# Moving the last full-array weight group of a squared-ReLU MLP to row tiles, and cutting the last output tile in two pieces in place of three

## The chip, the cores and the metric

The kernel runs on one core of a Trainium2 chip. The metric is the device time of one execution in microseconds (us), lower is better. One profiled execution gives a trace; its span is about 1.8 us less than the measured time of the same execution.

The lines of the profile use short names: PE is TensorE's matmuls, PEld its weight loads, ACT ScalarE, DVE VectorE, POOL GpSimd, SPq the DMA queue of SyncE; L182 is line 182 of the kernel.

## The reference

```python
B, S, D, F = 1, 2048, 576, 4608          # all bfloat16
h = einsum("bsd,df->bsf", x, w1) + b1    # contraction over D = 576
h = relu(h) ** 2
out = einsum("bsf,fd->bsd", h, w2) + b2  # contraction over F = 4608
```

## The kernel before

D = 576 is 4.5 times 128. A contraction over 576 therefore leaves a half slice of 64 rows. The kernel deals with it in two ways, and the change is about the choice between them.

The 2048 rows are four blocks of 512. The 4608 columns of w1 are 36 f-tiles of 128. For 32 of them the array is used as two *row tiles*: two f-tiles are computed at once, one on the upper 64 rows of the array and one on the lower 64, in nine slices of 64 each.

```python
def a_rows(sb, ...):                     # 16 groups of two f-tiles
    for j in range(NJ):                  # NJ = 16
        bx = ps_h.tile(...); by = ps_h.tile(...)
        for i in range(NC):              # NC = 9 slices of 64
            matmul(bx, lhsT=w1_h[0:H, LO_C[i], jc], rhs=xT[0:H, LO_W[i], :], ...)   # upper half
            matmul(by, lhsT=w1_h[H:P, UP_C[i], jc], rhs=xT[H:P, UP_W[i], :], ...)   # lower half
        evac_h(sb, bx, G + j)            # ScalarE: relu(x + b1); VectorE: square -> hT
        evac_h(sb, by, G + NJ + j)
```

The other four f-tiles (G = 4) form the *full-array group*: four matmuls over 128 rows for each f-tile, and the left-over 64 rows of two f-tiles as one pair of half-array matmuls.

```python
def a_full(sb, order):                   # four f-tiles
    def pair(i, start, stop):            # the left-over 64 rows of two f-tiles
        matmul(banks[2*i],   lhsT=w1n8[0:H, i, :], rhs=xT[0:H, SPC, :], ...)
        matmul(banks[2*i+1], lhsT=w1n8[H:P, i, :], rhs=xT[H:P, E3, :], ...)
    def full(g, k, start, stop):         # 128 rows
        matmul(banks[g], lhsT=w1n[:, k, g*P:(g+1)*P], rhs=xT[:, O + k, :], ...)
    # ... three orders: "k_outer" (block 0), "rows_first" (blocks 1, 3), "g_outer" (block 2)
```

The second product has two parts. `phase_t` makes output columns 512 to 575 of two blocks at once, with the array cut in two *column tiles* (128 rows by 64 columns). `phase_b` makes columns 0 to 511 with the full array. The very last tile of 128 output rows is cut by columns, so that its last addition and store are small.

```python
EDGES = [0, 224, 384, 512]
def phase_b(sb, hT, last=False, ...):
    for jj in range(RT):
        edges = EDGES if last and jj == RT - 1 else [0, DM]       # DM = 512
        for d0, d1 in zip(edges, edges[1:]):
            po = ps_o.tile(...)
            for i, ft in enumerate(ft_order):                     # 36 f-tiles
                matmul(po[:, 0:d1-d0], lhsT=hT[:, ft, jj*P:(jj+1)*P], rhs=w2_sb[:, ft, d0:d1], ...)
            tensor_tensor(out=o_sb[:, d0:d1], in0=po[:, 0:d1-d0], in1=b2_bc[:, d0:d1], op=add)
            dma_start(out=out2[rt*P:(rt+1)*P, d0:d1], in_=o_sb[:, d0:d1])
```

The order of the phases:

```python
a_full(0, "k_outer"); a_rows(0, 12, 1)
a_rows(1); a_full(1, "rows_first")
phase_t(0); phase_b(0, ...); phase_b(1, ...)
a_full(2, "g_outer"); a_rows(2)
a_rows(3); a_full(3, "rows_first")
phase_t(2); phase_b(2, ...); phase_b(3, ..., last=True)
```

Of the kernel before, what the change touches and what calls it, by code (L numbers as in the profile page):

```python
# [11 lines left out]
BF16 = mybir.dt.bfloat16  # L12
# [5 lines left out]
def kernel(  # L18
# [9 lines left out]
    nc = tc.nc  # L28
    keep = tc.keep_in_program_order
    P = 128  # L30
    H = 64
# [5 lines left out]
    NC = D // H  # L37
    NK = NC // 2
    G = 4
    GW = G * P  # L40
    NJ = (NFT - G) // 2
# [8 lines left out]
    wpool = ctx.enter_context(tc.tile_pool(name="wpool", bufs=1))  # L50
# [15 lines left out]
    w1n = wpool.tile([P, NK, GW], BF16, name="w1n")  # L66
    w1n8 = wpool.tile([P, G // 2, P], BF16, name="w1n8")
    w1_h = wpool.tile([P, NC, FH], BF16, name="w1_h")
    w1_v = w1.rearrange("(c p) f -> p c f", p=H)

    def load_x(eng, rt):
        keep(eng.dma_start(out=xs[:, rt, :], in_=x2[rt * P:(rt + 1) * P, :]))
# [8 lines left out]
    def load_w1(eng, h, j0, j1):  # L81
        keep(eng.dma_start(out=w1_h[h * H:(h + 1) * H, :, j0 * P:j1 * P],
                      in_=w1_v[:, :, GW + h * FH + j0 * P:GW + h * FH + j1 * P]))

    load_x(nc.sync, 0)
    load_x(nc.scalar, 1)
# [20 lines left out]
    E3, O, SPC, E = 0, 1, 5, 6  # L107
    LO_W = [O, O + 1, O + 2, O + 3, E, E + 1, E + 2, E3, SPC]
    LO_C = [0, 2, 4, 6, 1, 3, 5, 7, 8]
    UP_W = [O, O + 1, O + 2, O + 3, E3, E, E + 1, E + 2, SPC]  # L110
    UP_C = [1, 3, 5, 7, 8, 2, 4, 6, 0]
# [6 lines left out]
    def dup_windows(sb):  # L118
        xT = xT_blk[sb]
        keep(nc.vector.tensor_copy(out=xT[0:H, SPC:SPC + 4, :], in_=xT[H:P, E3:E3 + 4, :]))  # L120
        keep(nc.vector.tensor_copy(out=xT[H:P, SPC:SPC + 4, :], in_=xT[0:H, O:O + 4, :]))  # L121
# [34 lines left out]
    def make_b1T():  # L156
        b1T_ps = ps_o.tile([P, P], BF16, name="b1T_ps", tag="po")
        keep(nc.tensor.transpose(b1T_ps[:], b1_rows[:], ident[:]))  # L158
        keep(nc.vector.tensor_copy(out=b1T[:], in_=b1T_ps[:, 0:NFT]))
# [3 lines left out]
    def alloc_hT(sb):  # L163
        hTs[sb] = hpool.tile([P, NFT, SB], BF16, name="hT", tag="hT")

    def evac_h(sb, bank, ft):
        r = rpool.tile([P, SB], BF16, name="r", tag="r")
        keep(nc.scalar.activation(out=r[:], in_=bank[:], func=ACT.Relu, bias=b1T[:, ft:ft + 1], scale=1.0))  # L168
        keep(nc.vector.tensor_tensor(out=hTs[sb][:, ft, :], in0=r[:], in1=r[:], op=ALU.mult))  # L169

    def a_rows(sb, dup_at=None, dup_sb=None):
        xT = xT_blk[sb]
        for j in range(NJ):
            if j == dup_at:
                dup_windows(dup_sb)
            bx = ps_h.tile([P, SB], FP32, name="ph", tag="ph")
            by = ps_h.tile([P, SB], FP32, name="ph", tag="ph")
            jc = slice(j * P, (j + 1) * P)
            for i in range(NC):
                keep(nc.tensor.matmul(bx[:], lhsT=w1_h[0:H, LO_C[i], jc], rhs=xT[0:H, LO_W[i], :],  # L180
                                 start=(i == 0), stop=(i == NC - 1)))
                keep(nc.tensor.matmul(by[:], lhsT=w1_h[H:P, UP_C[i], jc], rhs=xT[H:P, UP_W[i], :],  # L182
                                 start=(i == 0), stop=(i == NC - 1)))
            evac_h(sb, bx, G + j)
            evac_h(sb, by, G + NJ + j)

    def a_full(sb, order):
        xT = xT_blk[sb]
        banks = []
        for g in range(G):  # L190
            pool, tag = (ps_o, "po") if g < 2 else (ps_h, "ph")
            banks.append(pool.tile([P, SB], FP32, name="pn", tag=tag))

        def pair(i, start, stop):
            keep(nc.tensor.matmul(banks[2 * i][:], lhsT=w1n8[0:H, i, :], rhs=xT[0:H, SPC, :],  # L195
                             start=start, stop=stop))
            keep(nc.tensor.matmul(banks[2 * i + 1][:], lhsT=w1n8[H:P, i, :], rhs=xT[H:P, E3, :],  # L197
                             start=start, stop=stop))

        def full(g, k, start, stop):  # L200
            keep(nc.tensor.matmul(banks[g][:], lhsT=w1n[:, k, g * P:(g + 1) * P], rhs=xT[:, O + k, :],  # L201
                             start=start, stop=stop))

        if order == "rows_first":
            for i in (1, 0):
                pair(i, True, False)
            for g in (2, 3, 0, 1):
                for k in range(NK):
                    full(g, k, False, k == NK - 1)
                evac_h(sb, banks[g], g)  # L210
        else:
            if order == "k_outer":
                for k in range(NK):
                    for g in range(G):
                        full(g, k, k == 0, False)
                    if k == 1:
                        make_b1T()
            else:
                for g in (2, 3, 0, 1):
                    for k in range(NK):  # L220
                        full(g, k, k == 0, False)
            for i in (1, 0):
                pair(i, False, True)
                evac_h(sb, banks[2 * i], 2 * i)
                evac_h(sb, banks[2 * i + 1], 2 * i + 1)

    ft_order = list(range(G))
    for j in range(NJ):
        ft_order += [G + j, G + NJ + j]

    t_order = ft_order[G:] + ft_order[:G]
    EDGES = [0, 224, 384, 512]

    def phase_t(sb):
        pt = ps_o.tile([P, SB], FP32, name="pt", tag="po")
        for i, ft in enumerate(t_order):
            for h in range(2):
                keep(nc.tensor.matmul(pt[h * DT:(h + 1) * DT, :], lhsT=w2_sb[:, ft, DM:D], rhs=hTs[sb + h][:, ft, :],  # L238
                                      start=(i == 0), stop=(i == NFT - 1)))
        oT = tpool.tile([P, SB], BF16, name="oT", tag="oT")  # L240
        keep(nc.scalar.activation(out=oT[:], in_=pt[:], func=ACT.Identity, bias=b2T[:], scale=1.0))  # L241
        ot = tpool.tile([P, RT, P], BF16, name="ot", tag="ot")
        keep(nc.sync.dma_start_transpose(out=ot[:, :, :], in_=oT[:, :]))
        for h in range(2):
            r0 = (sb + h) * SB
            dst = out2[r0:r0 + SB, DM:D].rearrange("(j p) d -> p j d", p=P)
            keep(nc.sync.dma_start(out=dst, in_=ot[:, :, h * DT:(h + 1) * DT]))

    def phase_b(sb, hT, last=False, dups=()):
        for jj in range(RT):  # L250
# [3 lines left out]
            o_sb = opool.tile([P, DM], BF16, name="o_sb", tag="o_sb")  # L254
            edges = EDGES if last and jj == RT - 1 else [0, DM]
            for d0, d1 in zip(edges, edges[1:]):
# [7 lines left out]
    for (j0, j1) in [(0, 1), (1, 2), (2, 4), (4, 6), (6, 8), (8, 10), (10, 12)]:  # L264
        load_w1(nc.sync, 0, j0, j1)
        load_w1(nc.sync, 1, j0, j1)
    load_xT(1)
    for (j0, j1) in [(12, 14), (14, 16)]:
        load_w1(nc.sync, 0, j0, j1)
        load_w1(nc.sync, 1, j0, j1)  # L270
    keep(nc.sync.dma_start(out=b2_bc[:], in_=b2.partition_broadcast(P)))
    for c in (0, 3, 1, 4, 2, 5):
        load_w2(c)
    load_xT(2)

    alloc_hT(0)
    a_full(0, "k_outer")
    a_rows(0, 12, 1)
    alloc_hT(1)
    load_xT(3)  # L280
    a_rows(1)
    a_full(1, "rows_first")
    phase_t(0)
    phase_b(0, hTs[0], dups=(2, 3))
    phase_b(1, hTs[1])
    alloc_hT(2)
    a_full(2, "g_outer")
    a_rows(2)
    alloc_hT(3)
    a_rows(3)  # L290
    a_full(3, "rows_first")
    phase_t(2)
    phase_b(2, hTs[2])
    phase_b(3, hTs[3], last=True)
# [30 lines left out]
```

## Time and profile before

| | before |
|---|---|
| time, first three runs | 291.56 us median (291.02 to 291.71) |
| span of the profiled run | 289.7 us |
| TensorE matmul busy | 285.7 us, 99% |
| ScalarE, VectorE busy | 95.7 us, 79.7 us |
| chain of waits | 98% TensorE |

These are lines of the page of the kernel before: busy time of each engine, then the chain of work that ended last, then the costliest groups (line, engine, operation, output<-inputs, shape, count | busy us, mean ns of one | idle time before them).

```profile
span 289.7 us, 4742 instructions
PE 285.7 (99%) x2052; PEld 134.1 (46%) x2052; DVE 79.7 (28%) x175; ACT 95.7 (33%) x156; POOL 4.2 (1%) x13
...
PE 98%; ACT 0%; DVE 0%; issue 0%
...
L182 PE MATMUL ph<-xTw,w_h 64*128 64x512 bf16 x576 | 124.6, 376 | 0.0
L180 PE MATMUL ph<-xTw,w_h 64*128 64x512 bf16 x576 | 124.6, 376 | 0.0
```

TensorE is the bound and has no idle time to fill. The two row-tile groups show how such a page has to be read: both are busy for 124.6 us, but at the same time. A matmul is listed with 376 ns, but the next one on the same half starts 0.22 us after it (below); what counts is the time from one start to the next. So the timeline is the view for this kernel. Its columns are the start in us, the duration, the engine, the line, the instruction (output<-inputs, shape) and how many are merged in the line; square brackets give the idle time before it and what ended that. In the kernel before, at the end of block 1's row tiles:

```profile
72.16 0.38 PE L195 MATMUL pn<-xTw,w1n_92 64*128 64x512 bf16 x1
72.16 0.38 PE L197 MATMUL pn<-xTw,w1n_92 64*128 64x512 bf16 x1
72.38 0.38 PE L195 MATMUL pn<-xTw,w1n_92 64*128 64x512 bf16 x1
72.38 0.38 PE L197 MATMUL pn<-xTw,w1n_92 64*128 64x512 bf16 x1
72.69 0.60 PE L201 MATMUL pn<-xTw,w1n 128*128 128x512 bf16 x2
...
75.72 0.59 PE L201 MATMUL pn<-xTw,w1n 128*128 128x512 bf16 x2
76.25 0.41 PE L238 MATMUL pt<-hT,w_sb 128*64 128x512 bf16 x2
```

Two halves start together, and the next pair 0.22 us later (72.16, 72.38). Where the layout of the array changes, the next start comes after 0.31 us: from row tiles to the full array at 72.38 to 72.69, and again from the full array (the second of the two at 75.72, so about 75.94) to column tiles at 76.25.

The tail of the same run, in the timeline of all engines:

```profile
279.04 0.69 DVE L261 TENSOR_TENSOR o_sb<-po,b_bc 128x512 bf16<-128x512 f32 x1 [7.08 <-PE po L259]
...
282.49 0.39 DVE L261 TENSOR_TENSOR o_sb<-po,b_bc 128x224 bf16<-128x224 f32 x1 [2.76 <-PE po L259]
284.98 0.33 DVE L261 TENSOR_TENSOR o_sb<-po,b_bc 128x160 bf16<-128x160 f32 x1 [2.10 <-PE po L259]
286.99 0.29 DVE L261 TENSOR_TENSOR o_sb<-po,b_bc 128x128 bf16<-128x128 f32 x1 [1.69 <-PE po L259]
```

Each addition starts when the 36 matmuls of its piece are done. The three pieces therefore take 3.45, 2.49 and 2.01 us.

### The profile page before, as it was taken

To read this page: it belongs to the slowest core of one execution; us is meant where nothing else is said; L and a number is where in the kernel's file an instruction comes from. 1 tells how busy PE (TensorE), PEld (TensorE's weight loads), DVE (VectorE), ACT (ScalarE), POOL (GpSimd) and SP (SyncE) were. 2 spreads that over 40 slices of the span, in tenths; PEclk is the share of its full clock that TensorE was granted. 3 is DMA by queue.
4 is the path that set the end of the run, shared out by engine and by line. 5 is a ranking of instruction groups with operands and counts; after the bars stand their busy time and mean duration, and the time that the engine had idled before them with its cause. 6 is when DMAs were issued, how large, how long until landed. Compare 5 with 4: busy or idle time off the path is not lost.

```text
span 289.7 us, 4742 instructions
## 1 busy us (share of the span) xinstructions
PE 285.7 (99%) x2052; PEld 134.1 (46%) x2052; DVE 79.7 (28%) x175; ACT 95.7 (33%) x156; POOL 4.2 (1%) x13
## 2 busy tenths in 40 slices
PE   8999999999999999999999999999999999999996
PEld 4444444444444444444444444444445444444475
DVE  3444554444502100000025444444440000000001
ACT  4566666666500000000027666666670000000000
POOL 5000000000000000000000000000000000000000
PEclk9999999999999999999999999999999999999999
DMA  7999999400001000000000000000000100000000
GB/s 205 253 227 208 316 391 157 95 0 2 0 20 36 0 18 20 18 18 18 20 18 2 1 2 0 2 0 2 0 2 0 36 20 18 18 18 20 18 20 20
DMA packets 30501, 16.26 MB, mean 56 GB/s; under 512 B 14692, under 2 KB 30448, under 8 KB 30480
## 3 DMA queue, kind: packets, MB, share of 16 engines
q1 hardware_dynamic: 30032, 15.59, 22.4%
q8 instruction: 16, 0.26, 0.4%
q10 hardware_dynamic: 288, 0.30, 0.3%
q0 software_dynamic: 160, 0.08, 0.1%
q14 instruction: 5, 0.04, 0.0%
HBM read 11.36 MB, written 2.36 MB: 47 GB/s over the span
## 4 chain that ended last, share of the span: by engine, by line
PE 98%; ACT 0%; DVE 0%; issue 0%
PE po L259 43%; PE ph L180 42%; PE pt L238 5%; PE pn L201 5%; PE wps L63 1%; PE ph L182 1%; PE pn L195 1%; PE ta L145 0%; ACT xTw L150 0%; ACT xTw L151 0%; DVE o_sb L261 0%; PE tb L149 0%; PE tb L148 0%; PE b1T_ps L158 0%; PE pn L197 0%
## 5 line engine op out<-in xcount | busy, mean ns | idle before, releaser
L259 PE MATMUL po<-w_sb,hT 128*128 128x512 bf16 (+3 forms) x648 | 124.8, 355 | 0.0
L182 PE MATMUL ph<-xTw,w_h 64*128 64x512 bf16 x576 | 124.6, 376 | 0.0
L180 PE MATMUL ph<-xTw,w_h 64*128 64x512 bf16 x576 | 124.6, 376 | 0.0
L168 ACT ACTIVATE r<-ph,b1T 128x512 bf16<-128x512 f32 x128 | 81.1, 685 | 41.6 <-PE ph L182 41.6
L259 PEld LDWEIGHTS <-hT 128*128 128x128 bf16 x648 | 60.7, 98 | 64.3 <-issue 0.8
L180 PEld LDWEIGHTS <-w_h 64*128 64x128 bf16 x576 | 54.1, 94 | 68.3
L169 DVE TENSOR_TENSOR hT<-r 128x512 bf16<-128x512 bf16 x144 | 61.3, 426 | 77.3 <-ACT r L168 76.9
L182 PEld LDWEIGHTS <-w_h 64*128 64x128 bf16 x576 | 54.1, 94 | 0.0
L261 DVE TENSOR_TENSOR o_sb<-po,b_bc 128x512 bf16<-128x512 f32 (+3 forms) x18 | 11.4, 633 | 125.0 <-PE po L259 125.0
L168 ACT ACTIVATE r<-pn,b1T 128x512 bf16<-128x512 f32 x16 | 10.3, 688 | 70.5 <-PE pn L197 69.2
L238 PE MATMUL pt<-hT,w_sb 128*64 128x512 bf16 x144 | 15.9, 380 | 0.0
L201 PE MATMUL pn<-xTw,w1n 128*128 128x512 bf16 x64 | 14.5, 379 | 0.4 <-ACT xTw L150 0.4
L238 PEld LDWEIGHTS <-w_sb 128*64 128x64 bf16 x144 | 8.0, 110 | 7.8 <-issue 0.8
L201 PEld LDWEIGHTS <-w1n 128*128 128x128 bf16 x64 | 6.0, 98 | 8.2 <-issue 1.4
L241 ACT ACTIVATE oT<-pt,b2T 128x512 bf16<-128x512 f32 x2 | 1.4, 687 | 14.5 <-PE pt L238 14.5
L63 PE MATMUL wps<-const-bfloat16-1.0 128*128 128x512 bf16 (+1 forms) x7 | 2.9, 594 | 0.8 <-PEq L309 0.8
L120 DVE COPY xTw<-xTw 64x2048 bf16<-64x2048 bf16 x4 | 2.8, 690 | 0.4 <-ACT xTw L151 0.3
L121 DVE COPY xTw<-xTw 64x2048 bf16<-64x2048 bf16 x4 | 2.7, 686 | 0.1
L146 DVE COPY xTw<-ta 128x384 bf16<-128x384 bf16 x4 | 1.4, 358 | 4.5 <-PE ta L145 4.3
L195 PE MATMUL pn<-xTw,w1n_92 64*128 64x512 bf16 x8 | 2.4, 379 | 0.0
L197 PE MATMUL pn<-xTw,w1n_92 64*128 64x512 bf16 x8 | 2.4, 379 | 0.0
L63 PEld LDWEIGHTS <-const-bfloat16-1.0 128*128 128x128 bf16 x7 | 0.9, 135 | 2.1 <-issue 2.1
(26 smaller groups left out, 16.1 us busy)
## 6 DMA issues: line engine op xcount, KB each, us to landing
w_sb<-in_w_dram SPq DMA_DIRECT2D x6, 864.0 KB, 10.6
w_h<-in_w_dram SPq DMA_DIRECT2D x14, 288.0 KB, 6.3
out_dram<-o_sb SPq DMA_DIRECT2D x15, 128.0 KB, 1.7
w_h<-in_w_dram SPq DMA_DIRECT2D x4, 144.0 KB, 3.5
w1n<-in_w_dram SPq DMA_DIRECT2D x4, 128.0 KB, 3.7
x_sb<-in_x_dram ACTq DMA_DIRECT2D x2, 144.0 KB, 3.2
x_sb<-in_x_dram SPq DMA_DIRECT2D x2, 144.0 KB, 2.9
out_dram<-ot SPq DMA_DIRECT2D x4, 64.0 KB, 1.9
```

The lines of the kernel that those rows point to most:

```text
L63: keep(nc.tensor.matmul(wps[:, 0:n], lhsT=ones[:, 0:P], rhs=ones[:, 0:n], start=True, stop=True))
L120: keep(nc.vector.tensor_copy(out=xT[0:H, SPC:SPC + 4, :], in_=xT[H:P, E3:E3 + 4, :]))
L121: keep(nc.vector.tensor_copy(out=xT[H:P, SPC:SPC + 4, :], in_=xT[0:H, O:O + 4, :]))
L168: keep(nc.scalar.activation(out=r[:], in_=bank[:], func=ACT.Relu, bias=b1T[:, ft:ft + 1], scale=1.0))
L169: keep(nc.vector.tensor_tensor(out=hTs[sb][:, ft, :], in0=r[:], in1=r[:], op=ALU.mult))
L180: keep(nc.tensor.matmul(bx[:], lhsT=w1_h[0:H, LO_C[i], jc], rhs=xT[0:H, LO_W[i], :], start=(i == 0), stop=(i == NC - 1)))
L182: keep(nc.tensor.matmul(by[:], lhsT=w1_h[H:P, UP_C[i], jc], rhs=xT[H:P, UP_W[i], :], start=(i == 0), stop=(i == NC - 1)))
L195: keep(nc.tensor.matmul(banks[2 * i][:], lhsT=w1n8[0:H, i, :], rhs=xT[0:H, SPC, :], start=start, stop=stop))
L201: keep(nc.tensor.matmul(banks[g][:], lhsT=w1n[:, k, g * P:(g + 1) * P], rhs=xT[:, O + k, :], start=start, stop=stop))
L238: keep(nc.tensor.matmul(pt[h * DT:(h + 1) * DT, :], lhsT=w2_sb[:, ft, DM:D], rhs=hTs[sb + h][:, ft, :], start=(i == 0), stop=(i == NFT - 1)))
L259: keep(nc.tensor.matmul(po[:, 0:d1 - d0], lhsT=hT[:, ft, jj * P:(jj + 1) * P], rhs=w2_sb[:, ft, d0:d1], start=(i == 0), stop=(i == NFT - 1)))
L261: keep(nc.vector.tensor_tensor(out=o_sb[:, d0:d1], in0=po[:, 0:d1 - d0], in1=b2_bc[:, d0:d1], op=ALU.add))
```

## The change

The intent is one way of working in place of two. The full-array group stays only in block 0, where it starts TensorE on the first weights to arrive. In blocks 1 to 3 the same four f-tiles run as two more row-tile groups; for that their weights are loaded a second time, in row-tile layout (`w1_x`). The last tile is cut into 384 and 128 columns in place of 224, 160 and 128.

```diff
+    w1_x = wpool.tile([P, NC, GW // 2], BF16, name="w1_x")
+    def load_w1x(eng, h):
+        keep(eng.dma_start(out=w1_x[h * H:(h + 1) * H, :, :], in_=w1_v[:, :, h * GW // 2:(h + 1) * GW // 2]))
     ...
     def a_rows(sb, dup_at=None, dup_sb=None):
-        for j in range(NJ):
+        pairs = [] if sb == 0 else [(w1_x, j, j, G // 2 + j) for j in range(G // 2)]
+        pairs += [(w1_h, j, G + j, G + NJ + j) for j in range(NJ)]
+        for n, (w, j, fa, fb) in enumerate(pairs):
     ...          # a_full: only the order "k_outer" is left
-    t_order = ft_order[G:] + ft_order[:G]        # phase_t now uses ft_order
-    EDGES = [0, 224, 384, 512]
+    EDGES = [0, 384, 512]
     ...          # after the loads of w1_h, ahead of b2 and w2:
+    for h in range(2):
+        load_w1x(nc.sync, h)
     ...
     a_rows(1)
-    a_full(1, "rows_first")
     phase_t(0)
     ...
-    a_full(2, "g_outer")
     a_rows(2)
     a_rows(3)
-    a_full(3, "rows_first")
     phase_t(2)
```

More of the change, by code (lines that the diff above doesn't have):

```diff
@@ L172, in a_rows @@
         xT = xT_blk[sb]
-        for j in range(NJ):
-            if j == dup_at:
+        pairs = [] if sb == 0 else [(w1_x, j, j, G // 2 + j) for j in range(G // 2)]
+        pairs += [(w1_h, j, G + j, G + NJ + j) for j in range(NJ)]
+        for n, (w, j, fa, fb) in enumerate(pairs):
+            if n == dup_at:
                 dup_windows(dup_sb)
@@ L179, in a_rows, with a_full @@
             for i in range(NC):
-                keep(nc.tensor.matmul(bx[:], lhsT=w1_h[0:H, LO_C[i], jc], rhs=xT[0:H, LO_W[i], :],
+                keep(nc.tensor.matmul(bx[:], lhsT=w[0:H, LO_C[i], jc], rhs=xT[0:H, LO_W[i], :],
                                  start=(i == 0), stop=(i == NC - 1)))
-                keep(nc.tensor.matmul(by[:], lhsT=w1_h[H:P, UP_C[i], jc], rhs=xT[H:P, UP_W[i], :],
+                keep(nc.tensor.matmul(by[:], lhsT=w[H:P, UP_C[i], jc], rhs=xT[H:P, UP_W[i], :],
                                  start=(i == 0), stop=(i == NC - 1)))
-            evac_h(sb, bx, G + j)
-            evac_h(sb, by, G + NJ + j)
-    def a_full(sb, order):
+            evac_h(sb, bx, fa)
+            evac_h(sb, by, fb)
+    def a_full(sb):
         xT = xT_blk[sb]
@@ L192, in a_full @@
             banks.append(pool.tile([P, SB], FP32, name="pn", tag=tag))
-        def pair(i, start, stop):
+        for k in range(NK):
+            for g in range(G):
+                keep(nc.tensor.matmul(banks[g][:], lhsT=w1n[:, k, g * P:(g + 1) * P], rhs=xT[:, O + k, :],
+                                 start=(k == 0), stop=False))
+            if k == 1:
+                make_b1T()
+        for i in (1, 0):
             keep(nc.tensor.matmul(banks[2 * i][:], lhsT=w1n8[0:H, i, :], rhs=xT[0:H, SPC, :],
-                             start=start, stop=stop))
+                             start=False, stop=True))
             keep(nc.tensor.matmul(banks[2 * i + 1][:], lhsT=w1n8[H:P, i, :], rhs=xT[H:P, E3, :],
-                             start=start, stop=stop))
-        def full(g, k, start, stop):
-            keep(nc.tensor.matmul(banks[g][:], lhsT=w1n[:, k, g * P:(g + 1) * P], rhs=xT[:, O + k, :],
-                             start=start, stop=stop))
-        if order == "rows_first":
-            for i in (1, 0):
-                pair(i, True, False)
-            for g in (2, 3, 0, 1):
-                for k in range(NK):
-                    full(g, k, False, k == NK - 1)
-                evac_h(sb, banks[g], g)
-        else:
-            if order == "k_outer":
-                for k in range(NK):
-                    for g in range(G):
-                        full(g, k, k == 0, False)
-                    if k == 1:
-                        make_b1T()
-            else:
-                for g in (2, 3, 0, 1):
-                    for k in range(NK):
-                        full(g, k, k == 0, False)
-            for i in (1, 0):
-                pair(i, False, True)
-                evac_h(sb, banks[2 * i], 2 * i)
-                evac_h(sb, banks[2 * i + 1], 2 * i + 1)
+                             start=False, stop=True))
+            evac_h(sb, banks[2 * i], 2 * i)
+            evac_h(sb, banks[2 * i + 1], 2 * i + 1)
     ft_order = list(range(G))
@@ L229 @@
         ft_order += [G + j, G + NJ + j]
-    t_order = ft_order[G:] + ft_order[:G]
-    EDGES = [0, 224, 384, 512]
+    EDGES = [0, 384, 512]
     def phase_t(sb):
         pt = ps_o.tile([P, SB], FP32, name="pt", tag="po")
-        for i, ft in enumerate(t_order):
+        for i, ft in enumerate(ft_order):
             for h in range(2):
@@ L276 @@
     alloc_hT(0)
-    a_full(0, "k_outer")
+    a_full(0)
     a_rows(0, 12, 1)
```

## The prediction

> **What bounds the kernel now.** TensorE. The page gives PE 285.7 of 289.7 us busy (99%), and the chain of waits is 98% PE; ACT is 33% busy, DVE 28%, and their idle sums in the waits view are waits for PE. The granted clock is full. From 5.96 to 287 us the timeline shows matmuls starting at a fixed pitch, so the time is a count of slots: a 128x512 matmul starts every 0.216 us, and so does a pair of 64-row matmuls on the two halves of the array (block 0, 10.00 to 41.08 us: 144 pairs, 0.2158 us each). The 376 ns of one matmul is latency, not cost.
>
> **What the change removes and adds.** In blocks 1 to 3 four f-tiles move from the full-array group (16 full matmuls and 2 pairs, 18 slots) to two row-tile groups (2 x 9 pairs, 18 slots): 3.9 us per block either way. There are 16 more matmuls per block, at no cost: the second of a pair starts with the first.
>
> 1. *Switches of array layout.* The Trainium skill, "TensorEngine Tiling (Array Packing)", Key Properties, says that changing the tiling mode drains the TensorE. The trace agrees: at each change the start-to-start gap is 0.31 us in place of 0.216 (72.38 to 72.69 rows to full; about 75.93 to 76.25 full to column tiles; to 84.14 column tiles to full; to 149.86 full to rows), a cost of about 0.095 us. Before has 8 such changes after the warm-up; after has 6, since rows go straight to the column-tiled phase in blocks 1 and 3. Saving 2 x 0.095 = 0.19 us, all critical.
> 2. *Last tile.* 224+160+128 becomes 384+128. The DVE starts in the tail (279.04, 282.49, 284.98, 286.99) give 36 matmuls in 3.45, 2.49 and 2.01 us: 95.8, 69.2, 55.8 ns each, i.e. 0.417 ns a column plus about 2.5 ns. A 384-column one is estimated at 162.5 ns: 5.85 us in place of 5.94, 0.09 us saved. The last piece keeps 128 columns, so the last addition (293 ns) and store (1.5 us) stay.
> 3. *Loads.* Two more loads of 288 KB on the SP queue, after the last row-tile weights (issued to 25.5 us). Comparable ones land in 3.3 to 7.3 us: there by about 34 us; block 1 needs them at 41.3. They push the w2 loads back by about 2 us, needed only from 76 us. Not critical.
> 4. *Evictions.* Two banks per 1.94 us need 2 x 0.69 = 1.37 us of ACT, as now. The last row pair of blocks 1 and 3 is used last in the 7.9 us column-tiled phase.
>
> **Prediction.** 291.56 - 0.19 - 0.09 = 291.3 us; the three runs of before spread 0.7. I say **291.25 us, 290.7 to 291.75**. Faster by over 2%: 0.005; within 2%: 0.985; slower by over 2%: 0.01.
>
> **What would show it.** Row pairs still at 0.216 us in blocks 1 to 3; one 0.31 us gap where rows meet column tiles; block 1 (41 to 76 us) 0.1 us shorter; the tail from the last full tile to the last addition 0.09 us shorter; no PE wait on a DMA at the start of block 1.
>
> **What would make it wrong.** The new weights landing after 41 us and stalling TensorE; a costlier change straight from row to column tiles than via the full array; the 384 piece's store colliding with the last one (a 224-column store took 3.1 us, the other two 1.5).

## The result and the profile after

| | runs | median us (lowest to highest) | before, same rounds | ratio (95% interval) |
|---|---|---|---|---|
| first measurement | 5 | 291.39 (291.37 to 291.60) | 291.71 (291.02 to 291.91) | 0.9995 (0.9981 to 1.0008) |
| again, five rounds | 5 | 291.27 (290.82 to 291.35) | 291.46 (291.22 to 292.01) | 0.9985 (0.9973 to 0.9998) |

A ratio is from the runs of both kernels in the same rounds, so it is not quite the ratio of the medians quoted beside it. The ratios further down are to the kernel before as well. By the threshold of 2% the two kernels are the same. The second measurement puts the changed kernel just clear of no change; the first does not.

The page of the changed kernel:

```profile
span 289.8 us, 4754 instructions
PE 285.3 (98%) x2052; PEld 132.3 (46%) x2064; DVE 79.4 (27%) x174; ACT 95.4 (33%) x156; POOL 4.0 (1%) x13
...
PE 98%; issue 0%; DVE 0%; ACT 0%
...
L186 PE MATMUL ph<-xTw,w_x 64*128 64x512 bf16 x54 | 12.1, 376 | 0.0
L188 PE MATMUL ph<-xTw,w_x 64*128 64x512 bf16 x54 | 12.1, 376 | 0.0
...
w_x<-in_w_dram SPq DMA_DIRECT2D x2, 288.0 KB, 7.0
```

This page alone would mislead. Its span is 0.1 us *longer* than that of the kernel before. (It also lists 2052 matmuls beside 2064 weight loads: twelve matmul records are missing.) The timeline shows what it hides. The start of block 1, then the border to the column-tiled phase:

```profile
41.33 0.38 PE L186 MATMUL ph<-xTw,w_h 64*128 64x512 bf16 x1
41.33 0.38 PE L188 MATMUL ph<-xTw,w_h 64*128 64x512 bf16 x1
41.54 0.38 PE L186 MATMUL ph<-xTw,w_x 64*128 64x512 bf16 x1
41.54 0.38 PE L188 MATMUL ph<-xTw,w_x 64*128 64x512 bf16 x1
...
76.07 0.38 PE L186 MATMUL ph<-xTw,w_h 64*128 64x512 bf16 x1
76.08 0.38 PE L188 MATMUL ph<-xTw,w_h 64*128 64x512 bf16 x1
76.29 0.38 PE L186 MATMUL ph<-xTw,w_h 64*128 64x512 bf16 x1
76.29 0.38 PE L188 MATMUL ph<-xTw,w_h 64*128 64x512 bf16 x1
76.60 0.41 PE L223 MATMUL pt<-hT,w_sb 128*64 128x512 bf16 x2
```

The first groups on the new weights keep the pace (41.33 to 41.54), with no wait. There is one gap of 0.31 us (76.29 to 76.60) where there were two. The tail of the changed kernel, in the timeline of all engines:

```profile
279.29 0.69 DVE L246 TENSOR_TENSOR o_sb<-po,b_bc 128x512 bf16<-128x512 f32 x1 [7.08 <-PE po L244]
285.14 0.56 DVE L246 TENSOR_TENSOR o_sb<-po,b_bc 128x384 bf16<-128x384 f32 x1 [5.16 <-PE po L244]
287.15 0.29 DVE L246 TENSOR_TENSOR o_sb<-po,b_bc 128x128 bf16<-128x128 f32 x1 [1.45 <-PE po L244]
```

The last tile's matmuls take 5.85 + 2.01 = 7.86 us in place of 3.45 + 2.49 + 2.01 = 7.95.

**A measure that does not depend on the start.** In every trace I took the start of the first row-tile matmul of block 0, of the first column-tiled matmul of blocks 1 and 3, and of the last addition. The differences between them are free of what happens in the first 10 us, and the unrounded starts resolve a nanosecond.

| us | before | before, second trace | after | after, second trace |
|---|---|---|---|---|
| first row tile to first column tile | 66.245 | 66.244 | 66.138 | 66.138 |
| from there to the column tiles of blocks 2 and 3 | 140.300 | 140.299 | 140.193 | 140.193 |
| from there to the last addition | 70.444 | 70.445 | 70.354 | 70.355 |
| **stretch, sum of the three** | **276.989** | **276.988** | **276.685** | **276.686** |
| first row tile starts at | 10.00 | 9.69 | 10.46 | 9.93 |
| full clock granted from | 4.97 | 4.03 | 6.71 | 4.41 |

The change gains 0.304 us: 0.107 in the first part, 0.107 in the second, 0.090 in the tail. Each repeats to 1 or 2 ns. The profiled run of the changed kernel lost more than that before its first row tile, which came at 10.46 us in place of 10.00, and this is why its span is longer.

**What moves the start.** The last line of the table is read from the trace's clock records. The timelines show the same. In the second trace of the changed kernel the 128-column transposes first come 0.11 us apart and then 0.055:

```profile
3.82 0.31 PE L152 MATMUL tb<-ident,x_sb 128*128 128x128 bf16 x1
3.93 0.31 PE L153 MATMUL tb<-ident,x_sb 128*128 128x128 bf16 x1
...
4.67 0.22 PE L152 MATMUL tb<-ident,x_sb 128*128 128x128 bf16 x1
4.72 0.22 PE L153 MATMUL tb<-ident,x_sb 128*128 128x128 bf16 x1
```

The Trainium skill, "TensorE: Matmul & The Clock Gate", Part 1, says that the array starts at half clock and is released after a window of about 3.4 us of activity, that this window runs freely, and so the moment varies from run to run. The traces agree: in the twelve traces that hold the record (all but the one of "rows_only", below), the release came between 3.38 and 6.71 us, in no visible relation to the kernel, and then the full clock lasted 283.31, 286.72, 290.13 or 296.96 us (but for "wx_late"), lengths that differ by multiples of 3.41 us. The five traces with a release before 4.5 us have their first row tile at 9.68 to 9.93 us, the five after 6 us at 10.35 to 10.53, and the two between at 10.00 and 10.21. The clock is not the whole of it: the first transpose starts at 3.50 us in some traces and as late as 3.91 in others (there, in "wx_late", 0.20 us of it is a wait for the load of x), and the second trace of the changed kernel waits 0.6 us for a weight load. These shares were not separated. The scatter of 0.85 us lies under every time in this document and is nearly three times the effect of the change.

### The profile page after: what moved, and what is told of

It reads as the page before. It is cut to its first block, busy times and chain, and to the rows that moved or that the text cites. A ratio compares the mean times of both kernels' runs of the same rounds, so it can differ in the third digit from the quotient of the medians.

```text
span 289.8 us, 4754 instructions
## 1 busy us (share of the span) xinstructions
PE 285.3 (98%) x2052; PEld 132.3 (46%) x2064; DVE 79.4 (27%) x174; ACT 95.4 (33%) x156; POOL 4.0 (1%) x13
## 4 chain that ended last, share of the span: by engine, by line
PE 98%; issue 0%; DVE 0%; ACT 0%
PE ph L186 46%; PE po L244 43%; PE pt L223 5%; PE pn L201 1%; PE wps L63 1%; PE ph L188 1%; PE ta L149 0%; PE pn L206 0%; PE tb L153 0%; PE tb L152 0%; DVE o_sb L246 0%; ACT xTw L154 0%; PE b1T_ps L162 0%; PE pn L208 0%
## 5 line engine op out<-in xcount | busy, mean ns | idle before, releaser
L244 PE MATMUL po<-w_sb,hT 128*128 128x512 bf16 (+2 forms) x600 | 124.0, 366 | 0.7 <-issue 0.2
L172 ACT ACTIVATE r<-ph,b1T 128x512 bf16<-128x512 f32 x140 | 88.5, 683 | 109.5 <-PE ph L188 109.5
L244 PEld LDWEIGHTS <-hT 128*128 128x128 bf16 x612 | 58.3, 98 | 66.6 <-issue 0.8
L246 DVE TENSOR_TENSOR o_sb<-po,b_bc 128x512 bf16<-128x512 f32 (+2 forms) x17 | 11.2, 660 | 123.9 <-PE po L244 116.8
L186 PE MATMUL ph<-xTw,w_x 64*128 64x512 bf16 x54 | 12.1, 376 | 0.0
L188 PE MATMUL ph<-xTw,w_x 64*128 64x512 bf16 x54 | 12.1, 376 | 0.0
L186 PEld LDWEIGHTS <-w_x 64*128 64x128 bf16 x54 | 5.0, 94 | 6.6 <-issue 0.4
L188 PEld LDWEIGHTS <-w_x 64*128 64x128 bf16 x54 | 5.0, 94 | 0.0
L201 PE MATMUL pn<-xTw,w1n 128*128 128x512 bf16 x16 | 3.9, 397 | 0.3 <-ACT xTw L154 0.3
L172 ACT ACTIVATE r<-pn,b1T 128x512 bf16<-128x512 f32 x4 | 2.4, 688 | 4.1 <-PE pn L208 4.1
```

The costliest lines, as they stand in the source:

```text
L172: keep(nc.scalar.activation(out=r[:], in_=bank[:], func=ACT.Relu, bias=b1T[:, ft:ft + 1], scale=1.0))
L186: keep(nc.tensor.matmul(bx[:], lhsT=w[0:H, LO_C[i], jc], rhs=xT[0:H, LO_W[i], :], start=(i == 0), stop=(i == NC - 1)))
L188: keep(nc.tensor.matmul(by[:], lhsT=w[H:P, UP_C[i], jc], rhs=xT[H:P, UP_W[i], :], start=(i == 0), stop=(i == NC - 1)))
L201: keep(nc.tensor.matmul(banks[g][:], lhsT=w1n[:, k, g * P:(g + 1) * P], rhs=xT[:, O + k, :], start=(k == 0), stop=False))
L244: keep(nc.tensor.matmul(po[:, 0:d1 - d0], lhsT=hT[:, ft, jj * P:(jj + 1) * P], rhs=w2_sb[:, ft, d0:d1], start=(i == 0), stop=(i == NFT - 1)))
L246: keep(nc.vector.tensor_tensor(out=o_sb[:, d0:d1], in0=po[:, 0:d1 - d0], in1=b2_bc[:, d0:d1], op=ALU.add))
```

## The experiments

The measured columns are the stretch defined above and the time of the runs. "After" has a stretch of 276.685 us and "before" 276.989.

### The changed kernel again

No edit; five rounds.

> The changed kernel unaltered, timed again beside the kernel before. Theory (two layout switches and 36 small-matmul overheads less): the stretch from the first row-tile matmul of block 0 to the start of the last addition is again 276.7 us (277.0 in the kernel before), and the median is 0.1 to 0.5 us below before. Rival (the difference of the profiles is an accident of the start, where the clock is released at a different moment): the stretch is not reproducible to 0.1 us.

The stretch was 276.686 us, against 276.685 in the first trace. The median was 291.27 us against 291.46 of the kernel before (0.19 us lower, ratio 0.9985, interval 0.9973 to 0.9998). So the rival fell: the start moved by half a microsecond between the two traces of the changed kernel, and the stretch did not move.

### The kernel before again

No edit; one look.

> The kernel before, unaltered, for a second trace of it. Theory: the stretch from first row-tile matmul to last addition is 276.99 us again to within 0.02, while the start of the first row-tile matmul lies anywhere from 9.8 to 10.6 us, later when the full clock is granted later. Rival: the stretch itself varies by 0.1 us or more, and the 0.30 us between the kernels is not shown.

276.988 us, against 276.989. The first row tile came at 9.69 us, slightly earlier than the range that I gave; the full clock was granted at 4.03 us. The 0.304 us between the kernels are shown by two traces of each.

### Row tiles alone ("rows_only")

```diff
-    EDGES = [0, 384, 512]
+    EDGES = [0, 224, 384, 512]
```

> The changed kernel with the last tile cut in three again (224, 160, 128): row tiles alone. Theory: the stretch from first row-tile matmul to last addition is 277.0 - 0.19 = 276.8 us. Rival (the row tiles gain nothing, the whole 0.3 us comes from the last tile): 277.0.

The stretch was 276.775 us: 66.139 + 140.192 + 70.444. The first two parts are those of the changed kernel, the third is that of the kernel before. The row tiles are worth 276.989 - 276.775 = 0.214 us, 0.107 for each of the two layout changes taken away. The median time was 291.77 us (four runs, ratio 1.0001, interval 0.9987 to 1.0015): the times could not have shown this.

### The tail alone ("tail_only")

```diff
-    EDGES = [0, 224, 384, 512]
+    EDGES = [0, 384, 512]          # in the kernel before
```

> The kernel before with the last tile cut into 384 and 128: the tail alone. Theory: the stretch is 277.0 - 0.09 = 276.9 us and the last tile's matmuls take 7.85 us in place of 7.94. Rival: 276.7.

The stretch was 276.898 us: 66.243 + 140.300 + 70.355. The first two parts are those of the kernel before, the third is that of the changed kernel. The tail is worth 0.091 us, and 0.214 + 0.091 = 0.305 is the whole. The median was 291.57 us, ratio 0.9997 (0.9982 to 1.0013), again no help.

### Ninety-two layout changes more ("scattered")

The full-array matmuls of blocks 1 to 3 of the kernel before, spread over the row-tile groups in place of one run; their pairs come ahead of groups 0 and 8.

```diff
     def a_rows(sb, ...):
+        banks = [ps_o.tile([P, SB], FP32, name="pn", tag="po") for g in range(G)] if sb > 0 else []
         for j in range(NJ):
+            if sb > 0 and j % (2 * NK) == 0:      # the pair of half-array matmuls, start=True
+                ...
             ...                                   # the nine row-tile pairs of group j, as before
+            if sb > 0:
+                g, k = j // NK, j % NK
+                matmul(banks[g][:], lhsT=w1n[:, k, g*P:(g+1)*P], rhs=xT[:, O + k, :], ...)
     ...
-    a_full(1, "rows_first")       # and those of blocks 2 and 3
```

> The kernel before, with the 16 full-array matmuls of blocks 1 to 3 no longer in one run but one after each of the 16 row-tile groups, so that the array layout changes some 32 times in a block in place of 1 or 2: 92 changes more in all, with the same number of matmuls. Theory (each change costs 0.095 us): 92 x 0.095 = 8.7 us more, about 300.3 us. Rival (a change costs nothing by itself; the 0.31 us gaps are something that happens once at a phase border, such as a late semaphore): within 1 us of before.

The time was 301.17 us. The stretch was 286.775 us, 9.786 us more than before. The trace has 100 layout changes after the warm-up where before has 8, as intended (one of each lies ahead of the stretch). 9.786 / 92 = 0.1064 us for each, the same as the 0.107 in the change itself. The rival, that a gap belongs to a phase border, fell. But the cost per change is 0.011 us above the 0.095 that I had put down, and the timeline of TensorE shows why:

```profile
42.82 0.38 PE L187 MATMUL ph<-xTw,w_h 64*128 64x512 bf16 x1
42.82 0.38 PE L189 MATMUL ph<-xTw,w_h 64*128 64x512 bf16 x1
43.13 0.39 PE L195 MATMUL pn<-xTw,w1n 128*128 128x512 bf16 x1
43.45 0.39 PE L187 MATMUL ph<-xTw,w_h 64*128 64x512 bf16 x1
43.45 0.39 PE L189 MATMUL ph<-xTw,w_h 64*128 64x512 bf16 x1
43.68 0.38 PE L187 MATMUL ph<-xTw,w_h 64*128 64x512 bf16 x1
43.68 0.38 PE L189 MATMUL ph<-xTw,w_h 64*128 64x512 bf16 x1
43.89 0.38 PE L187 MATMUL ph<-xTw,w_h 64*128 64x512 bf16 x1
```

From row tiles to the full array takes 0.31 us (42.82 to 43.13), back takes 0.32 (43.13 to 43.45), and the first interval after that is 0.23 in place of 0.22 (43.45 to 43.68). In nanoseconds the trace gives 312, 322 and 227 against a steady 216. So a change costs 96 ns at once and 10 or 11 ns more in the interval that follows it, 106 in all (the 322 ns hold both: the second interval of one change is the first of the next). The same 226 or 227 ns follow the changes in the kernel before and in the changed kernel, except into column tiles, where both have 240; I had read only the first gap.

### The new weights loaded later ("wx_late")

```diff
-    for h in range(2):
-        load_w1x(nc.sync, h)
     keep(nc.sync.dma_start(out=b2_bc[:], ...))
     for c in (0, 3, 1, 4, 2, 5):
         load_w2(c)
+    for h in range(2):
+        load_w1x(nc.sync, h)
```

> The changed kernel with the two new weight loads issued after the six w2 loads in place of before them. Theory (the loads are free only because they land 7 us before block 1 wants them): issued at about 40 us and landing some 7 us later, they stop TensorE at the start of block 1 from 41.5 to about 47 us, and 5 to 8 us are lost for good: about 297 us. Rival (there is slack, work moves around it): within 1 us of the changed kernel.

The time was 301.64 us, a stretch of 286.949: 10.26 us lost, all of it in the first part. That is more than the 5 to 8 us expected. The timeline of TensorE at the start of block 1:

```profile
41.07 0.38 PE L188 MATMUL ph<-xTw,w_h 64*128 64x512 bf16 x1
49.42 0.60 PE L186 MATMUL ph<-xTw,w_x 64*128 64x512 bf16 x1 [7.97 <-DMA w_x<-in_w_dram]
50.30 0.60 PE L188 MATMUL ph<-xTw,w_x 64*128 64x512 bf16 x1 [0.28 <-DMA w_x<-in_w_dram]
50.30 0.61 PE L186 MATMUL ph<-xTw,w_x 64*128 64x512 bf16 x1
50.70 0.63 PE L188 MATMUL ph<-xTw,w_x 64*128 64x512 bf16 x1
...
52.83 0.39 PE L188 MATMUL ph<-xTw,w_x 64*128 64x512 bf16 x1
```

The two loads took 9.6 and 10.9 us to land behind the w2 loads, in place of 6.7 and 7.3, and the wait was 8.1 us longer than a slot of 0.216 us. The rest, some 2.1 us, is the second load's wait and the clock: the trace has half clock from 46.02 to 52.85 us, and the pairs come 0.4 us apart until then. The Trainium skill, "TensorE: Matmul & The Clock Gate", Part 1, says that an idle window of about 3.4 us puts the array back to half clock; here the clock fell 4.95 us after the last matmul had started (41.07 to 46.02). So the rival fell: a late load is lost for good, with interest. In the changed kernel the loads were issued at 25.9 and 26.9 us and landed by about 34, some 7 us ahead of their use at 41.5.

### Nine upper halves, then nine lower ones ("unpaired")

```diff
-            for i in range(NC):
-                matmul(bx, upper half i); matmul(by, lower half i)
+            for i in range(NC): matmul(bx, upper half i)      # only the groups on w1_x
+            for i in range(NC): matmul(by, lower half i)
```

> The changed kernel with the matmuls of the first two row-tile groups of blocks 1 to 3 in another order: nine on the upper half of the rows, then nine on the lower half, in place of alternating. The same matmuls and weights. Theory (a pair costs one slot because its second matmul starts with its first, and matmuls start in order): only neighbours of different halves overlap, 15 slots of 0.216 us are lost in each block, 9.7 us in all, about 301 us. Rival (the array overlaps the halves whatever their order): no change.

Neither theory held. The time was 294.21 us and the stretch 279.898, so 3.2 us were lost in place of 9.7 or none. The timeline of TensorE, where L187 is the upper half and L190 the lower:

```profile
40.90 1.46 PE L187 MATMUL ph<-xTw,w_x 64*128 64x512 bf16 x6
41.99 0.39 PE L190 MATMUL ph<-xTw,w_x 64*128 64x512 bf16 x1
42.20 0.38 PE L187 MATMUL ph<-xTw,w_x 64*128 64x512 bf16 x1
42.22 0.38 PE L190 MATMUL ph<-xTw,w_x 64*128 64x512 bf16 x1
42.41 0.38 PE L187 MATMUL ph<-xTw,w_x 64*128 64x512 bf16 x1
42.43 0.38 PE L190 MATMUL ph<-xTw,w_x 64*128 64x512 bf16 x1
```

Six upper matmuls start alone or nearly so, and then the first lower one starts at 41.99 us, although three upper ones that precede it in the program start only at 42.20, 42.41 and 42.63. The instructions are compiled in the order of the program: the kernel has nine L187, then nine L190 in TensorE's instructions. So TensorE took a matmul ahead of three earlier ones, which were still to pass the other half of the array. The same happens where the halves change next, at 43.09 and 44.19 us: six have started and three are left.

### Threes ("threes")

The same, in chunks of three upper and three lower matmuls.

> The changed kernel with the matmuls of the first two row-tile groups of blocks 1 to 3 in threes: three on the upper half of the rows, three on the lower half, three upper, and so on. In the run with nines the first lower matmul started while three upper ones that precede it in the program had not started. Theory now (TensorE starts a matmul ahead of up to three earlier ones that wait for the other half): in threes nothing is lost, the stretch from first row-tile matmul to last addition stays within 0.3 us of the changed kernel's 276.69. Rival (strict order of starts, with something else behind the small loss with nines): 3 slots lost in each of 6 groups, 3.9 us, stretch 280.6 us.

The stretch was 276.692 us, 6 ns from the changed kernel. Strict order would have cost 3.9 us. In the timeline each lower matmul starts with its upper one. This supports the reading of the run with nines: matmuls on different halves overlap if their distance in the program is small. With nines the first lower matmul stood behind nine upper ones, and started only when three of them were left to pass; with threes it had two to pass, and did so at once. What exactly sets that limit was not measured further.

### The last tile as 448 and 64 ("tail_64")

```diff
-    EDGES = [0, 384, 512]
+    EDGES = [0, 448, 512]
```

> The changed kernel with the last tile cut into 448 and 64 columns. Theory A (0.417 ns a column plus 2.5 ns also at 64 columns): 36 last matmuls in 1.05 us, the same matmul time in all (7.86 us) and a last addition about 0.07 us shorter, so 0 to 0.1 us better. Theory B (a 128-column weight load, 98 ns long and twice as frequent here, sets a floor near 50 to 56 ns a matmul): the last 36 take 1.8 to 2.0 us and the kernel is 0.7 to 1.0 us slower.

Theory A held. The stretch was 276.686 us, unchanged to 1 ns, and the last 36 matmuls took 1.05 us, 29.2 ns each. The 98 ns weight load ahead of each is no floor. The last addition took 0.22 us in place of 0.29: these 0.07 us are shown. The span ended 2.56 us after the start of that addition in place of 2.67, but that end holds a store, and with other kernels it varies by 0.4 us (below), so the rest of the 0.11 us is not shown. The median was 291.33 us, ratio 0.9995 (0.9980 to 1.0010): the times don't show the gain.

### The last tile as 480 and 32 ("tail_32")

```diff
-    EDGES = [0, 384, 512]
+    EDGES = [0, 480, 512]
```

> The changed kernel with the last tile cut into 480 and 32 columns. If 0.417 ns a column plus 2.5 ns holds down to 32 columns, the last 36 matmuls take 36 x 15.8 = 0.57 us; with the floor of 25 ns that the Trainium skill states (TensorE: Matmul & The Clock Gate) they take 0.90 us; if the time from one start to the next were bound by the weight load (98 ns) they would take 3.5 us. The first piece takes 36 x 202.5 = 7.29 us.

The last 36 matmuls took 0.89 us, 25 ns from start to start, which is the floor that the Trainium skill states ("TensorE: Matmul & The Clock Gate", Part 1); 0.417 ns a column no longer holds. The first piece took 7.29 us, and the stretch was 277.007 us, 0.32 worse than the changed kernel. The addition is then only 0.03 us shorter than with 64 columns. The one time, 291.04 us, is the lowest of the three kernels that ran together, but its full clock came at 3.96 us, which hides the 0.32.

### The last tile in one piece ("tail_one")

```diff
-    EDGES = [0, 384, 512]
+    EDGES = [0, 512]
```

> The changed kernel with the last tile in one piece of 512 columns. Theory: the matmuls take 7.77 us in place of 7.85, but the last addition takes 0.69 us in place of 0.29 and the last store carries 128 KB in place of 32 (1.7 us in place of 1.5): 0.3 to 0.6 us slower than the changed kernel. Rival (small pieces are worth nothing in the end): within 0.1 us.

The stretch was 276.594 us, 0.09 shorter as computed, but the span ended 3.37 us after the start of the last addition in place of 2.67. Together that is 0.61 us worse in these two traces, just above the 0.3 to 0.6 expected; 0.40 of it is the longer addition (0.69 us in place of 0.29). The median was 292.01 us. In the same rounds the kernel cut at 448 had 291.33, and its highest run (291.41) was below the lowest here (291.51). The rival fell: a small last piece is worth something.

## Why the prediction was right

The prediction was 291.25 us, with 290.7 to 291.75 as the range; the medians are 291.39 and 291.27. That the time fell into the range shows little by itself: the kernel before, at 291.46 to 291.71 in the same rounds, lies in it too, and the start alone moves by 0.85 us. What shows the mechanism is the stretch. The steps, one by one:

- *The time is a count of slots, and the change saves none.* Shown. Row pairs come every 0.216 us (215.8 ns on average) in all blocks of both kernels, and 16 full matmuls plus two pairs cost the same as 18 row pairs. "rows_only" leaves no room for another net gain or loss beyond 2 x 0.107 us.
- *Two layout changes less, 0.095 us each.* The mechanism was right; this is the term that was mis-sized. A change cost 0.1064 us in "scattered" and 0.107 in the change. The missing 0.011 us is the interval after the gap. The Trainium skill's statement that a mode change drains TensorE ("TensorEngine Tiling (Array Packing)", Key Properties) led to the right place; the price had to be read from the trace. That the gap is a drain is the page's word: the runs show its length and that it comes with every change.
- *Last tile, 0.09 us.* 0.090 us, shown by "tail_only". The rule of 0.417 ns a column plus about 2.5 ns, read from three sizes, gave 5.85 us for the 384-column piece, and 5.85 were measured. The skill's "TensorE: Matmul & The Clock Gate" gives the same form, N / 2.4 GHz plus 2.5 ns once warm.
- *The new loads are not critical.* Shown both ways: no wait in the changed kernel, 10.26 us lost when they were loaded later. The w2 loads were issued until 40.0 us in place of 38.7, so pushed back by 1.3 us and not by 2; it made no difference.
- *Straight from row tiles to column tiles might be dearer.* It was not: 309 ns, the same as from the full array.
- *The store of the 384-column piece might collide with the last.* No store of the changed kernel took more than 2.1 us, and the end came 2.67 us after the last addition's start, against 2.75 before; other traces of kernels with the same last piece show 2.67 to 3.10, so nothing can be read from this difference.

The sum is 0.304 us against 0.28 predicted. What the times alone could not decide, two things did: cutting the uncertain first 10 us out of the comparison, and multiplying the disputed cost by 46.

## What to carry to other kernels

When the bounding engine is fully busy, count its slots before and after: here a rewrite that kept the number of slots kept the time, and what remained was the price of the seams, 0.106 us for every change between row tiles and the full array, so order phases so that equal layouts meet. For gains of a tenth of a per cent, compare stretches between two fixed instructions in the traces rather than spans or times, after finding out what jitters at the start. Ahead of a load that a stage depends on, look at its margin and not only at its bandwidth: 7 us of margin cost nothing, and losing it cost 10 us.

## What the Trainium skill lacked or had wrong

- "TensorEngine Tiling (Array Packing)", Key Properties, says that a mode change drains TensorE but gives no price. Here a change between row tiles and the full array cost 0.106 us: 311 to 312 ns from start to start in place of 216, and about 227 in the next interval. Into column tiles the two intervals were 309 and 240 ns, the same from row tiles as from the full array; from column tiles to the full array 315 and 226.
- "TensorE: Matmul & The Clock Gate", Part 3, What overlaps and what doesn't, says that matmuls start and end strictly in program order. In "unpaired" a lower-half matmul started at 41.99 us ahead of three upper-half ones that precede it in the program (42.20, 42.41, 42.63), and "threes" lost 0.006 us where strict order would have cost 3.9 us.
- The same page, Back-to-back issue gap, gives 81 ns a matmul for 128 columns and 131 ns for 512 in a stream of weight loads and matmuls, and calls N / 2.4 GHz plus 2.5 ns the isolated gap. Here, with a new weight load ahead of every matmul, the stream ran at 55.8 ns for 128 columns, 29.2 for 64, and 216 for 512: here the formula that the page calls isolated is the sustained one. Its floor of about 25 ns was confirmed at 32 columns.
- The same page, Part 1, puts the variation of the clock's release at ±500 ns from run to run. Here matmuls began at 0.77 or 0.78 us in every trace, went on with short pauses for data, and the release came anywhere from 3.38 to 6.71 us.
